# Routing attention and a squared-ReLU feed-forward: moving the rounding of `w_out` between the additions of the first feed-forward

## The chip, the cores and the metric

The kernel runs on one core of a Trainium2 chip. The metric is device time in microseconds (us). The core has a matmul engine (PE, with its weight loads shown as PEld), a vector engine (DVE), an activation engine (ACT), a general engine (POOL) and SP, a sequencer that here only issues DMAs. Each engine works through its own queue in order, and waits on semaphores for the others.

## The reference, cut to what matters

Two blocks follow each other. The first is attention in which a query sees only the keys of its own cluster; the second is a feed-forward whose activation is a squared ReLU:

```python
attn_out = _attn_ref(q, k, v, centroids)            # 4 batches, 8 heads, 768 rows, 64 wide
x = attn_out.transpose(0, 2, 1, 3).reshape(3072, 512)
h = x @ w_in                                        # w_in  512 x 2048
g = np.maximum(h, 0.0) ** 2
out = g @ w_out                                     # w_out 2048 x 512
```

The change concerns only the second block, and there only the first of its four batches.

## The kernel before

**Stages.** The attention runs over 16 pairs of heads (the loop over `p`). Then each of four batches, in the order 1, 2, 3, 0 (`FEED`), goes through `up` (x times `w_in`, squared ReLU, result in the tile `g`) and `down` (`g` times `w_out`, result in `osb` and out).

**Seven products instead of eight.** Both `up` and `down` split their operands into 2 x 2 parts and use a scheme with seven products of sums. `combine` (line 680) runs it: product 1 goes to a PSUM bank and ACT copies it out (line 698); then for products 6, 2, 7, 5, 4, 3 in this order PE fills one bank each, and DVE adds the bank into the result with seven operations (line 694 for the additions, line 520 for the one subtraction, product 4). There are eight banks, used in turn, so PE may be at most eight banks ahead of the engine that empties them. `up` has eight groups `i` of seven products; each product is four matmuls, issued as f32 (line 735). `down` has three groups `i` for each batch; each product is eight matmuls (line 787).

**Sums that the products need.** `w_sums(i)` (line 535) makes four sums `s1` to `s4` of parts of `w_in` on POOL, two groups ahead in the first `up`. Products 5, 6, 7 and 3 of group `i` read `s1`, `s2`, `s3`, `s4`. `w_out_sum(1..4)` (line 761) makes four sums of `w_out` on DVE, once, in the first group of the first `down`. `down` makes two sums of `g`, `s1` and `s2`, and overwrites two quarters of `g` by differences, on DVE.

**Rounding the weights.** Both weight matrices come as 64-bit words that are rounded to a 32-bit form in blocks of 128 x 512. Block `n` takes a DMA into a staging buffer `w_raw` (line 120, on SP's queue), two operations on ACT (`round_1`, lines 128 and 129), three on DVE (`round_2`, lines 135, 138 and 142), and one addition on POOL (`round_3`, line 150). Blocks 0 to 15 are `w_in`, 16 to 31 `w_out`. The attention loop rounds blocks 0 to 14. Block 15 and all of `w_out` are rounded inside the first `up`. There are three staging buffers, and `load_ahead(r)` issues the loads of all blocks below r + 3; a load waits until POOL is done with the block that had its buffer.

**Order.** From the start to the end of the first group of the first `down`, the order on PE, DVE, ACT, POOL and SP is the order of the program (`manual_schedule`). In the first `up`, `rounding(i, 1)` comes behind ACT's copy of product 1 and the squares of the group before: it queues `round_1` for three blocks in groups 0 and 1, for two in the others. `rounding(i, 2)` comes behind all additions of a group (and behind `w_sums(i + 2)` on POOL): it queues `round_2` and `round_3` of the same blocks one after the other, and the next loads. In group 0 it first adds up the last pair's softmax sums (`add_up` on PE, `invert` on DVE, a DMA out and back by `invert` and `spread`, and `finish` on DVE, line 508, which waits for that DMA). `check_sums` (lines 815 to 821) reads all those sums once; its DVE part is placed by the scheduler, and stands right behind `invert` in this trace.

In the other `up`s there is no rounding; DVE does most squares, and `w_sums(i)` is made with its group.

Of the kernel before, what the change touches and what calls it, by code (L numbers as in the profile page):

```python
# [12 lines left out]
U32 = mybir.dt.uint32  # L13
# [5 lines left out]
P = 128  # L19
# [6 lines left out]
def kernel(  # L26
# [18 lines left out]
    FT = DFF // P  # L45
    HP = H // 2
    NB = NCH // 2
    TB = NB * P
# [63 lines left out]
            weights.append((w_in[:, a, cols], w_in64[:, a, cols]))  # L112
    N_IN = len(weights)
    raw_w = {}

    def load_weights(i):
        if i < N_IN + FT:
            src = weights[i][1] if i < N_IN else w_out64[:, i - N_IN]
            raw_w[i] = wstage.tile([P, NW, 2], U32, name="w_raw")
            nc.sync.dma_start(raw_w[i], src)  # L120

    def of_block(i):
# [349 lines left out]
    def add_up(pair, bank):  # L472
        rows = P // 4
        for e in range(2):
            for g in range(2):
                nc.tensor.matmul(  # L476
                    bank[rows * (2 * e + g) : rows * (2 * e + g + 1), 0:TB], lhsT=ups[:, 0:rows],
                    rhs=total[pair][:, e, TB * g : TB * (g + 1)], start=True, stop=True,
                )
        total.pop(pair)  # L480
        sums[pair] = bank
# [37 lines left out]
    def sub(out, a, b, eng=nc.vector):  # L519
        return eng.tensor_tensor(out=out, in0=a, in1=b, op=ALU.subtract)  # L520
# [33 lines left out]

    def load_ahead(rounded):
        nonlocal loaded
        while loaded < min(rounded + 3, N_IN + FT):
            load_weights(loaded)
            loaded += 1

# [96 lines left out]
                    first_sums.append(found)  # L657
            w_early.append(w_sums(len(w_early)))
    att.close()
    load_ahead(NG - 1)  # L660

    w_out_pool = ctx.enter_context(tc.tile_pool(name="w_out_pool", bufs=1, reuse_waits="tile"))

# [2 lines left out]
    banks = fast.enter_context(tc.tile_pool(name="banks", bufs=8, space=PSUM, reuse_waits="tile"))  # L666
    outp = fast.enter_context(tc.tile_pool(name="outp", bufs=2, reuse_waits="tile"))
    gp = fast.enter_context(tc.tile_pool(name="gp", bufs=1, reuse_waits="tile"))

    def bank_tile(width):  # L670
        return banks.tile([P, width], F32, name="bank", tag="bank")
# [5 lines left out]
    ]  # L677
    w_t = {}

    def combine(c, product, width, early=(), behind_copy=None):  # L680
        (c11, c12), (c21, c22) = c
        waiting = {}

        def bank_of(j):
            if j in waiting:
                return waiting[j]
            bank = bank_tile(width)
            product(j, bank)
            return bank

        def add(j, *results):
            bank = bank_of(j)
            for out, to in results:
                nc.vector.tensor_tensor(out=out, in0=bank, in1=to, op=ALU.add)  # L694

        bank = bank_tile(width)
        product(1, bank)
        nc.scalar.copy(out=c11, in_=bank)  # L698
        if behind_copy:
            behind_copy()  # L700
        for j in early:
            waiting[j] = bank_of(j)
        add(6, (c12, c11))
        add(2, (c11, c11))
        add(7, (c21, c12))
        add(5, (c22, c21), (c12, c12))
        sub(c21, c21, bank_of(4))
        add(3, (c12, c12))
# [11 lines left out]
    def up(b, g, rounding=None):  # L720
        with tc.issue_after(last_w_sum[0]) if b == FEED[1] else ExitStack():
            x, t1, t2, t3, t4 = first_sums.pop() if first_sums else list(x_sums(b))[-1]
        waiting = []
        for i in range(F2):
            if rounding is None:
                w_early.append(w_sums(i))
            a, s1, s2, s3, s4 = w_early.pop(0)
            operands = {
                1: (a[0][0], x[0][0]), 2: (a[0][1], x[1][0]), 3: (s4, x[1][1]), 4: (a[1][1], t4),
                5: (s1, t1), 6: (s2, t2), 7: (s3, t3),  # L730
            }

            def product(j, bank):
                for kk in range(H2):
                    nc.tensor.matmul(  # L735
                        bank, lhsT=operands[j][0][:, kk], rhs=operands[j][1][:, kk],
                        start=(kk == 0), stop=(kk == H2 - 1),
                    )

            def behind_copy():  # L740
                if waiting:
                    squares(waiting.pop(), True)
                rounding(i, 1)

            c = [[g[:, f, h] for h in range(2)] for f in (i, F2 + i)]
            combine(c, product, TB, behind_copy=rounding and behind_copy)
            if rounding is None:
                squares(c, False)
                continue
            if i + 1 < F2:  # L750
                waiting.append(c)
            else:
                squares(c, False)
            if i + 2 < F2:
                w_early.append(w_sums(i + 2))
            rounding(i, 2)
        xT.pop(b)

    last_w_sum = [None]

    def w_out_sum(i):
        one, two = {1: (w_q[0][1], w_q[0][0]), 2: (w_q[1][1], w_t.get(1)),
                    3: (w_q[1][1], w_q[0][1]), 4: (w_t.get(2), w_q[1][0])}[i]
        w_t[i] = wtp.tile([P, F2, M2], F32, name=f"w_t{i}")
        last_w_sum[0] = sub(w_t[i], one, two).ins

    def down(b, g):
        for i in range(NB):
            begins = b == FEED[0] and i == 0
            cols = slice(i * P, (i + 1) * P)  # L770
            a = [[g[:, F2 * g2 : F2 * (g2 + 1), h, cols] for g2 in range(2)] for h in range(2)]
            s1, s2 = (sp.tile([P, F2, P], F32, name=f"g_s{j}", tag=f"s{j}") for j in (1, 2))
            nc.vector.tensor_tensor(out=s1, in0=a[1][0], in1=a[1][1], op=ALU.add)
            sub(s2, s1, a[0][0])
            if begins:
                w_out_sum(1)
            else:
                sub(a[1][0], a[0][0], a[1][0])

            def product(j, bank):  # L780
                left, right = {
                    1: (a[0][0], w_q[0][0]), 2: (a[0][1], w_q[1][0]), 3: (a[0][1], w_q[1][1]),
                    4: (a[1][1], w_t.get(4)), 5: (s1, w_t.get(1)), 6: (s2, w_t.get(2)),
                    7: (a[1][0], w_t.get(3)),
                }[j]
                for f in range(F2):
                    nc.tensor.matmul(  # L787
                        bank, lhsT=left[:, f], rhs=right[:, f], start=(f == 0), stop=(f == F2 - 1)
                    )
                if j == 2:  # L790
                    sub(a[0][1], a[0][1], s2)
                    if begins:
                        w_out_sum(2)
                        sub(a[1][0], a[0][0], a[1][0])
                if j == 3 and begins:
                    w_out_sum(3)
                    w_out_sum(4)

            osb = [outp.tile([P, DM], F32, name="osb") for _ in range(2)]
            c = [[osb[h][:, M2 * m : M2 * (m + 1)] for m in range(2)] for h in range(2)]  # L800
            combine(c, product, M2, early=(2, 3) if begins else (2, 4))
            if begins:
                manual.close()
                check_sums()
            last = b == FEED[-1] and i == NB - 1
            for h in (1, 0):
                for cols in (slice(0, M2), slice(M2, DM)) if last and h == 0 else (slice(0, DM),):
                    nc.sync.dma_start(out_view[b, h * NB + i][:, cols], osb[h][:, cols])
# [13 lines left out]
            out=flag[0:1], in0=every, scalar1=UP * float(rows * NG * NBL), scalar2=None, op0=ALU.is_lt  # L822
        )

    to_round = list(range(N_IN - 1, N_IN + FT))

    def rounding(i, stage):
        if stage == 2 and i == 0:
            add_up(NG - 1, bank_tile(TB))
            invert(NG - 1)  # L830
            spread(NG - 1)
            finish(NG - 1)
        if stage == 2 and i == 1:
            ending.close()
        blocks = to_round[: 3 if i < 2 else 2]
        if stage == 1:
            for n in blocks:
                if n >= N_IN:
                    round_1(n)
            return  # L840
        for n in blocks:
            round_2(n)
            round_3(n)
            load_ahead(n + 1)
        del to_round[: len(blocks)]

    for n, b in enumerate(FEED):
        g = gp.tile([P, FT, 2, TB], F32, name="g")
        up(b, g, None if n else rounding)
        if n == 0:  # L850
            staging.close()
            wtp = fast.enter_context(
                tc.tile_pool(name="wtp", bufs=1, side="right", reuse_waits="tile")
            )
            xT[0] = xp.tile([P, KT, S], F32, name="xT")
            nc.sync.dma_start(xT[0], x_far)
        down(b, g)
        if n == 0:
            again = nc.values_load(flag[0:1, 0:1], min_val=0, max_val=1)
# [191 lines left out]
```

## Time and profile before

| what | before |
|---|---|
| median of 3 runs | 919.5 us (919.38 to 921.3) |
| the profiled execution, its own time | 917.96 us |
| its span in the trace | 916.2 us, so 1.8 us lie outside it |
| PE / PEld / DVE / ACT / POOL busy | 98% / 63% / 63% / 34% / 16% |
| attention | start to 320.8 us |
| first `up` | 320.80 to 399.15 us: 56 products of PE and one small sum |
| first group of the first `down` | 399.15 to 427.41 us |
| second `up` | from 475.98 us |

Busy shares are means over the span. A view by stages shows more: of the first feed-forward, ten slices of 10 us each have

```profile
core 0: us, PE busy (x) PEld busy (x) DVE busy (x) ACT busy (x) POOL busy (x), PEclk, DMA share, GB/s
320.00:330.00 10.00, 10.00 (x37) 5.52 (x32) 5.82 (x8) 3.22 (x6) 5.26 (x5) 1.00 0.16 52
330.00:340.00 10.00, 10.00 (x38) 5.64 (x38) 4.53 (x10) 4.23 (x9) 2.82 (x4) 1.00 0.13 40
340.00:350.00 10.00, 6.93 (x17) 3.65 (x16) 9.65 (x15) 2.49 (x4) 7.35 (x7) 0.83 0.46 159
350.00:360.00 10.00, 10.00 (x32) 5.81 (x31) 9.58 (x17) 7.87 (x16) 7.23 (x7) 1.00 0.46 143
...
390.00:400.00 10.00, 10.00 (x33) 6.08 (x32) 9.55 (x19) 7.65 (x16) 3.28 (x3) 1.00 0.26 90
400.00:410.00 10.00, 6.28 (x30) 5.10 (x28) 9.83 (x12) 0.37 (x1) 2.20 (x1) 1.00 0.45 158
```

Each row is a stretch of the span; the columns are its length, then busy time and instructions of each engine, the clock that PE was granted (1.00 is full), and the DMA engines' share and rate. DVE is half idle up to 340 us and then busy without a break; PE is short of work in two of the slices, and its clock is below 1.00 in one.

### The profile page before, as it was taken

To read this page: it belongs to the slowest core of one execution; us is meant where nothing else is said; L and a number is where in the kernel's file an instruction comes from. 1 tells how busy PE (TensorE), PEld (TensorE's weight loads), DVE (VectorE), ACT (ScalarE), POOL (GpSimd) and SP (SyncE) were. 2 spreads that over 40 slices of the span, in tenths; PEclk is the share of its full clock that TensorE was granted. 3 is DMA by queue.
4 is the path that set the end of the run, shared out by engine and by line. 5 is a ranking of instruction groups with operands and counts; after the bars stand their busy time and mean duration, and the time that the engine had idled before them with its cause. 6 is when DMAs were issued, how large, how long until landed. Compare 5 with 4: busy or idle time off the path is not lost.

```text
span 916.2 us, 11745 instructions
## 1 busy us (share of the span) xinstructions
PE 900.2 (98%) x4543; PEld 578.9 (63%) x4543; DVE 580.9 (63%) x930; ACT 315.3 (34%) x457; POOL 146.1 (16%) x168
## 2 busy tenths in 40 slices
PE   8999999999999999989999999999999999999997
PEld 5444444444444455558885568886558887557886
DVE  5798888888888959996326565224565333656321
ACT  5876677766775536830001110001110000111000
POOL 0000100001000347620022310013320003240000
PEclk9999999999999999999999999999999999999999
DMA  7677787777663114330000000000000000000000
GB/s 260 164 192 217 223 202 205 193 222 186 176 169 102 41 46 156 118 113 24 24 24 0 1 0 12 16 19 23 1 1 0 24 24 24 0 1 0 24 24 27
DMA packets 98482, 75.03 MB, mean 82 GB/s; under 512 B 54666, under 2 KB 89074, under 8 KB 98162
## 3 DMA queue, kind: packets, MB, share of 16 engines
q1 hardware_dynamic: 91474, 64.33, 24.7%
q10 hardware_dynamic: 6944, 9.86, 3.4%
q8 instruction: 38, 0.62, 0.3%
q14 instruction: 26, 0.21, 0.1%
HBM read 43.83 MB, written 19.34 MB: 69 GB/s over the span
## 4 chain that ended last, share of the span: by engine, by line
PE 92%; DVE 6%; issue 1%; DMA 1%; ACT 0%; POOL 0%; SPq 0%; DVEq 0%; POOLq 0%
PE bank L787 31%; PE bank L735 29%; PE sc L424 12%; PE av_a L457 9%; PE av_b L457 4%; PE sc L433 3%; PE sc L320 1%; PE sc L476 1%; DVE g L694 1%; DVE w_raw L138 1%; DVE w_raw L135 1%; DVE total L443 1%; PE sc L169 0%; DMA rb<-far_r 0%; DVE xT L508 0%
## 5 line engine op out<-in xcount | busy, mean ns | idle before, releaser
L694 DVE TENSOR_TENSOR g<-bank,g 128x384 f32<-128x384 f32 x192 | 103.2, 555 | 94.7 <-PE bank L735 91.3
L440 ACT ACTIVATE ex<-sc 128x1024 f32<-128x1024 f32 x144 | 144.4, 1026 | 39.0 <-PE sc L424 34.1
L424 PE MATMUL sc<-qkT 64*128 64x512 f32 (+1 forms) x768 | 150.6, 484 | 0.0
L787 PE MATMUL bank<-w_out,g 128*128 128x256 f32 x576 | 127.3, 379 | 3.7 <-DVE g L520 3.7
L787 PEld LDWEIGHTS bank<-w_out,g 128*128 128x128 f32 x576 | 109.2, 190 | 19.9 <-DVE g L520 4.1
L694 DVE TENSOR_TENSOR osb<-bank,osb 128x256 f32<-128x256 f32 x72 | 29.4, 422 | 134.6 <-PE bank L787 124.1
L735 PE MATMUL bank<-xT,w_in 128*128 128x384 f32 x256 | 93.9, 490 | 3.1 <-DVE g L694 3.1
L735 PE MATMUL bank<-xT,w_s 128*128 128x384 f32 x256 | 94.2, 491 | 0.0
L735 PE MATMUL bank<-x_t,w_s 128*128 128x384 f32 x256 | 93.0, 486 | 0.0
L424 PEld LDWEIGHTS sc<-qkT 64*128 64x128 f32 x768 | 65.9, 188 | 41.9 <-issue 30.1
L787 PE MATMUL bank<-w_t,g 128*128 128x256 f32 x384 | 86.8, 379 | 0.0
L787 PE MATMUL bank<-w_t,g_s 128*128 128x256 f32 x384 | 86.8, 379 | 0.0
L457 PE MATMUL av_a<-ex,v_raw 128*64 128x512 f32 x384 | 85.9, 596 | 0.0
L443 DVE TENSOR_TENSOR total<-total,ex 128x1024 f32<-128x1024 f32 x64 | 78.7, 1229 | 6.5
L540 POOL TENSOR_TENSOR w_s<-w_in 128x256 f32<-128x256 f32 x32 | 24.7, 772 | 347.2 <-PE bank L787 226.4
L698 ACT COPY osb<-bank 128x256 f32<-128x256 f32 x12 | 4.5, 373 | 219.1 <-PE bank L787 219.1
L787 PEld LDWEIGHTS bank<-w_t,g_s 128*128 128x128 f32 x384 | 73.0, 190 | 9.9
L787 PEld LDWEIGHTS bank<-w_t,g 128*128 128x128 f32 x384 | 73.0, 190 | 9.9
L698 ACT COPY g<-bank 128x384 f32<-128x384 f32 x32 | 15.3, 477 | 172.5 <-PE bank L735 172.5
L735 PEld LDWEIGHTS bank<-xT,w_in 128*128 128x128 f32 x256 | 48.3, 190 | 37.3 <-DVE g L694 4.0
L735 PEld LDWEIGHTS bank<-xT,w_s 128*128 128x128 f32 x256 | 49.2, 192 | 34.6 <-issue 1.2
L150 POOL TENSOR_TENSOR w_in<-w_in,w_raw 128x512 int32<-128x512 int32 x16 | 22.4, 1400 | 302.2 <-DVE w_in L142 285.8
(128 smaller groups left out, 1015.6 us busy)
## 6 DMA issues: line engine op xcount, KB each, us to landing
words<-flat SPq DMA_DIRECT2D x28, 384.0 KB
w_raw<-in_moe_w_in_dram SPq DMA_DIRECT2D x16, 512.0 KB
w_raw<-in_moe_w_out_dram SPq DMA_DIRECT2D x16, 512.0 KB
v_raw<-in_v_dram SPq DMA_DIRECT2D x16, 384.0 KB
rb<-far_r SPq DMA_DIRECT2D x32, 192.0 KB
out_dram<-osb SPq DMA_DIRECT2D x23, 256.0 KB
k_raw<-in_k_dram ACTq DMA_DIRECT2D x13, 384.0 KB
q_raw<-in_q_dram ACTq DMA_DIRECT2D x12, 384.0 KB
```

The costliest lines, as they stand in the source:

```text
L135: nc.vector.scalar_tensor_tensor(out=lo, in0=hi, scalar=0x80000000, in1=lo, op0=ALU.bitwise_and, op1=ALU.bitwise_or)
L150: nc.gpsimd.tensor_tensor(out=dst, in0=dst, in1=lo, op=ALU.add)
L424: nc.tensor.matmul(sc[i][:, e, cols], lhsT=qkT[pair][rows, NCH + c], rhs=qkT[pair][rows, n.start // P : n.stop // P], start=first, stop=no ...
L433: nc.tensor.matmul(sc[i][:, e, cols], lhsT=ohT[pair][rows, 1, c * P : (c + 1) * P], rhs=ohT[pair][rows, 0, columns(i)], start=first, stop= ...
L440: nc.scalar.activation(out=ex[i], in_=sc.pop(i), func=ACT.Exp, scale=SCALE)
L443: eng.tensor_tensor(out=out, in0=a, in1=b, op=ALU.add)
L457: nc.tensor.matmul(bank[D * e : D * (e + 1), 0 : n.stop - n.start], lhsT=raw_v[pair][:, e, c], rhs=ex[i][:, e, cols], start=c == 0, stop=c ...
L540: nc.gpsimd.tensor_tensor(out=s1, in0=a[1][0], in1=a[1][1], op=ALU.add)
L694: nc.vector.tensor_tensor(out=out, in0=bank, in1=to, op=ALU.add)
L698: nc.scalar.copy(out=c11, in_=bank)
L735: nc.tensor.matmul(bank, lhsT=operands[j][0][:, kk], rhs=operands[j][1][:, kk], start=(kk == 0), stop=(kk == H2 - 1),)
L787: nc.tensor.matmul(bank, lhsT=left[:, f], rhs=right[:, f], start=(f == 0), stop=(f == F2 - 1))
```

## The change

- **Blocks by group.** The 17 blocks are now three a group in groups 0 to 4 and two in group 5; groups 6 and 7 round none. `Rounding.between(i, j)` is called behind the addition of product `j`: the group's first block goes behind the addition of product 6, its second behind that of 7, its third behind that of 3. Each is `round_2`, `round_3` and the load for the block six further on.
- **`round_1` a group earlier.** `Rounding.prepare(i)`, at the place of the old first stage, queues ACT's part for the blocks of group i + 1 (in group 0 for those of groups 0 and 1).
- **Six staging buffers.** A second pool of three, `stage_2`, opens after the attention's pools are closed; blocks alternate between the pools in threes. `load_ahead` runs six blocks ahead from there on.
- **Moved tail of the attention.** `add_up`, `invert` and `spread` of the last pair stay behind group 0, now behind its three blocks; `finish` moves behind group 2.
- **`w_out`'s sums.** Sums 1, 2 and 3 are made in the first `up`, behind the additions (6, 7), (6, 3) and (7, 7) of (group, product); only sum 4 stays in the first `down`, behind product 2. The subtraction on `a[1][0]` comes there at once, as in the other groups.
- **The first `down`'s order on PE** is 1, 2, 5, 7, 3, 6, 4 instead of 1, 2, 3, 6, 7, 5, 4.

```diff
@@ -112,11 +112,13 @@
             weights.append((w_in[:, a, cols], w_in64[:, a, cols]))
     raw_w = {}
+    stage_2 = None
 
     def load_weights(i):
         if i < N_IN + FT:
             src = weights[i][1] if i < N_IN else w_out64[:, i - N_IN]
-            raw_w[i] = wstage.tile([P, NW, 2], U32, name="w_raw")
+            pool = stage_2 if i > N_IN and (i - N_IN + 1) // 3 % 2 else wstage
+            raw_w[i] = pool.tile([P, NW, 2], U32, name="w_raw")
             nc.sync.dma_start(raw_w[i], src)
 
     def of_block(i):
@@ -554,7 +556,7 @@
 
     def load_ahead(rounded):
         nonlocal loaded
-        while loaded < min(rounded + 3, N_IN + FT):
+        while loaded < min(rounded + (6 if stage_2 else 3), N_IN + FT):
             load_weights(loaded)
             loaded += 1
 
@@ -657,7 +659,6 @@
                     first_sums.append(found)
             w_early.append(w_sums(len(w_early)))
     att.close()
-    load_ahead(NG - 1)
 
     w_out_pool = ctx.enter_context(tc.tile_pool(name="w_out_pool", bufs=1, reuse_waits="tile"))
 
@@ -666,6 +667,10 @@
     banks = fast.enter_context(tc.tile_pool(name="banks", bufs=8, space=PSUM, reuse_waits="tile"))
     outp = fast.enter_context(tc.tile_pool(name="outp", bufs=2, reuse_waits="tile"))
     gp = fast.enter_context(tc.tile_pool(name="gp", bufs=1, reuse_waits="tile"))
+
+    staging_2 = ExitStack()
+    stage_2 = staging_2.enter_context(tc.tile_pool(name="stage_2", bufs=3, reuse_waits="tile"))
+    load_ahead(NG - 1)
 
     def bank_tile(width):
         return banks.tile([P, width], F32, name="bank", tag="bank")
@@ -677,7 +682,7 @@
     ]
     w_t = {}
 
-    def combine(c, product, width, early=(), behind_copy=None):
+    def combine(c, product, width, early=(), behind_copy=None, behind_add=None):
         (c11, c12), (c21, c22) = c
         waiting = {}
 
@@ -692,6 +697,8 @@
             bank = bank_of(j)
             for out, to in results:
                 nc.vector.tensor_tensor(out=out, in0=bank, in1=to, op=ALU.add)
+            if behind_add:
+                behind_add(j)
 
         bank = bank_tile(width)
         product(1, bank)
@@ -740,10 +747,13 @@
             def behind_copy():
                 if waiting:
                     squares(waiting.pop(), True)
-                rounding(i, 1)
+                rounding.prepare(i)
 
             c = [[g[:, f, h] for h in range(2)] for f in (i, F2 + i)]
-            combine(c, product, TB, behind_copy=rounding and behind_copy)
+            combine(
+                c, product, TB, behind_copy=rounding and behind_copy,
+                behind_add=rounding and (lambda j: rounding.between(i, j)),
+            )
             if rounding is None:
                 squares(c, False)
                 continue
@@ -753,7 +763,7 @@
                 squares(c, False)
             if i + 2 < F2:
                 w_early.append(w_sums(i + 2))
-            rounding(i, 2)
+            rounding.behind(i)
         xT.pop(b)
 
     last_w_sum = [None]
@@ -772,10 +782,7 @@
             s1, s2 = (sp.tile([P, F2, P], F32, name=f"g_s{j}", tag=f"s{j}") for j in (1, 2))
             nc.vector.tensor_tensor(out=s1, in0=a[1][0], in1=a[1][1], op=ALU.add)
             sub(s2, s1, a[0][0])
-            if begins:
-                w_out_sum(1)
-            else:
-                sub(a[1][0], a[0][0], a[1][0])
+            sub(a[1][0], a[0][0], a[1][0])
 
             def product(j, bank):
                 left, right = {
@@ -790,15 +797,11 @@
                 if j == 2:
                     sub(a[0][1], a[0][1], s2)
                     if begins:
-                        w_out_sum(2)
-                        sub(a[1][0], a[0][0], a[1][0])
-                if j == 3 and begins:
-                    w_out_sum(3)
-                    w_out_sum(4)
+                        w_out_sum(4)
 
             osb = [outp.tile([P, DM], F32, name="osb") for _ in range(2)]
             c = [[osb[h][:, M2 * m : M2 * (m + 1)] for m in range(2)] for h in range(2)]
-            combine(c, product, M2, early=(2, 3) if begins else (2, 4))
+            combine(c, product, M2, early=(2, 5, 7, 3) if begins else (2, 4))
             if begins:
                 manual.close()
                 check_sums()
@@ -822,36 +825,50 @@
             out=flag[0:1], in0=every, scalar1=UP * float(rows * NG * NBL), scalar2=None, op0=ALU.is_lt
         )
 
-    to_round = list(range(N_IN - 1, N_IN + FT))
-
-    def rounding(i, stage):
-        if stage == 2 and i == 0:
-            add_up(NG - 1, bank_tile(TB))
-            invert(NG - 1)
-            spread(NG - 1)
-            finish(NG - 1)
-        if stage == 2 and i == 1:
-            ending.close()
-        blocks = to_round[: 3 if i < 2 else 2]
-        if stage == 1:
-            for n in blocks:
+
+    class Rounding:
+        blocks = [[N_IN - 1 + 3 * i + j for j in range(3)] for i in range(F2)]
+
+        def of(self, i):
+            return [n for n in self.blocks[i] if n < N_IN + FT] if i < F2 else []
+
+        def prepare(self, i):
+            for n in self.of(i) + self.of(1) if i == 0 else self.of(i + 1):
                 if n >= N_IN:
                     round_1(n)
-            return
-        for n in blocks:
-            round_2(n)
-            round_3(n)
-            load_ahead(n + 1)
-        del to_round[: len(blocks)]
+
+        def between(self, i, j):
+            n = dict(zip((6, 7, 3), self.of(i))).get(j)
+            if n is not None:
+                round_2(n)
+                round_3(n)
+                load_ahead(n + 1)
+            elif (i, j) in SUMS:
+                w_out_sum(SUMS[i, j])
+
+        def behind(self, i):
+            nonlocal wtp
+            if i == 0:
+                add_up(NG - 1, bank_tile(TB))
+                invert(NG - 1)
+                spread(NG - 1)
+            if i == 2:
+                finish(NG - 1)
+            if i == 5:
+                staging_2.close()
+                ending.close()
+                staging.close()
+                wtp = fast.enter_context(
+                    tc.tile_pool(name="wtp", bufs=1, side="right", reuse_waits="tile")
+                )
+
+    SUMS = {(6, 7): 1, (6, 3): 2, (7, 7): 3}
+    wtp = None
 
     for n, b in enumerate(FEED):
         g = gp.tile([P, FT, 2, TB], F32, name="g")
-        up(b, g, None if n else rounding)
+        up(b, g, None if n else Rounding())
         if n == 0:
-            staging.close()
-            wtp = fast.enter_context(
-                tc.tile_pool(name="wtp", bufs=1, side="right", reuse_waits="tile")
-            )
             xT[0] = xp.tile([P, KT, S], F32, name="xT")
             nc.sync.dma_start(xT[0], x_far)
         down(b, g)
```

## The prediction

> **What bounds the kernel now.** I read the page's chain of waits first: it runs through PE for nine tenths of the span.
>
> ```profile
> PE 92%; DVE 6%; issue 1%; DMA 1%; ACT 0%; POOL 0%; SPq 0%; DVEq 0%; POOLq 0%
> ```
>
> So only time in which PE stands still or runs slowly can be won. The timeline of PE (start, us, operation, count, and in brackets the idle time before it and its releaser) says where that is, inside the stage that the change touches:
>
> ```profile
> 341.23 1.45 PE L735 MATMUL bank<-x_t,w_s 128*128 128x384 f32 x4
> 345.75 2.12 PE L735 MATMUL bank<-xT,w_in 128*128 128x384 f32 x4 [3.07 <-DVE g L694]
> 347.67 2.63 PE L735 MATMUL bank<-xT,w_s 128*128 128x384 f32 x4
> 350.13 1.46 PE L735 MATMUL bank<-x_t,w_s 128*128 128x384 f32 x4
> ...
> 399.15 7.07 PE L787 MATMUL bank<-w_out,g 128*128 128x256 f32 x32
> 409.95 3.72 PE L787 MATMUL bank<-w_out,g 128*128 128x256 f32 x16 [3.72 <-DVE g L520]
> ```
>
> A product of `up` begins every 1.29 us, one of `down` every 3.45. From 320.80 to 427.41 (106.6 us) PE has 56 products of the one (72.2), `add_up` (0.8) and 7 of the other (24.2): 97.2. It **loses 9.4 us**: 3.2 waiting for a bank at 342.5, 1.8 in the two products behind, which take 1.92 and 2.46 instead of 1.29 at a lower clock, 3.9 waiting for DVE's subtraction at 406, some 0.5 in handovers. After 427.41 nothing is left to win here.
>
> Both waits are DVE's. Its timeline has the first cause, and then a group of two blocks:
>
> ```profile
> 337.13 1.60 DVE L508 SCALAR_TENSOR_TENSOR xT<-xT,rb 128x384 f32<-128x384 f32 x2 [3.47 <-DMA rb<-far_r]
> ...
> 359.05 0.55 DVE L694 TENSOR_TENSOR g<-bank,g 128x384 f32<-128x384 f32 x1
> 359.52 1.24 DVE L135 SCALAR_TENSOR_TENSOR w_raw<-w_raw 128x512 uint32<-128x512 uint32 x1
> 360.80 0.43 DVE L138 TENSOR_SCALAR w_raw<-w_out 128x512 f32<-128x512 f32 x1
> 361.26 0.43 DVE L142 TENSOR_SCALAR w_out<-w_raw 128x512 uint32<-128x512 uint32 x1
> 361.61 0.69 DVE L135 SCALAR_TENSOR_TENSOR w_raw<-w_raw 128x512 uint32<-128x512 uint32 x1
> 362.33 1.40 DVE L138 TENSOR_SCALAR w_raw<-w_out 128x512 f32<-128x512 f32 x1
> 363.76 0.43 DVE L142 TENSOR_SCALAR w_out<-w_raw 128x512 uint32<-128x512 uint32 x1
> ```
>
> From 331.8 DVE waits 5.3 us for the reciprocals' DMAs (0.4 of it is L815), then rounds three blocks, and empties no bank until 345.15. From there it never idles. The same line takes 0.69 or 1.24, 0.43 or 1.40; POOL's timeline shows why.
>
> ```profile
> 357.29 0.73 POOL L540 TENSOR_TENSOR w_s<-w_in 128x256 f32<-128x256 f32 x1
> 358.10 0.73 POOL L520 TENSOR_TENSOR w_s<-w_s,w_in 128x256 f32<-128x256 f32 x1
> 358.79 0.73 POOL L520 TENSOR_TENSOR w_s<-w_in 128x256 f32<-128x256 f32 x1
> 359.48 0.73 POOL L520 TENSOR_TENSOR w_s<-w_in,w_s 128x256 f32<-128x256 f32 x1
> 361.77 1.67 POOL L150 TENSOR_TENSOR w_out<-w_out,w_raw 128x512 int32<-128x512 int32 x1 [1.56 <-DVE w_out L142]
> 364.27 1.30 POOL L150 TENSOR_TENSOR w_out<-w_out,w_raw 128x512 int32<-128x512 int32 x1 [0.82 <-DVE w_out L142]
> ```
>
> The L135 at 359.52 ends 0.55 late, as the last `w_s` sum runs; the L138 at 362.33 0.97 late, behind the L150 that slipped in between L135 and L138. They take turns, one instruction each. The adds out of PSUM (L694) don't suffer.
>
> **Prices on DVE.** Seven bank operations: 3.65 (355.87 to 359.52). A block alone: 0.72 + 0.46 + 0.35 = 1.53. Waits: 1.5 for two blocks, now.
>
> **The change, part by part.**
>
> *`finish` two groups later.* The 5.3 us of DVE idling go. SP's order matters: the loads of blocks 21, 22, 23 now stand ahead of the reciprocals' DMAs, and the last waits for block 17's L150 (about 334.2). By the 1.40, 0.45 and 3.31 us that the chain shows for these DMAs they land near 340; `finish` comes near 355, so that costs nothing. L815 needs the first of them, at about 336: between 0, if the scheduler puts it in a gap, and 2.4 us, if right behind `invert` as now. I take its 0.44, since what follows is no longer a wait for a DMA.
>
> *Rounding between the adds, three a group.* The first block now starts one add (0.54) behind the previous group's third, while POOL still has that block's L150 (1.30) and, behind it, four `w_s` sums. With turns taken, from the rows above: first block's L135 waits 0.83 for the L150, its L138 0.41 and its L142 0.44 for a `w_s` sum each; second block, two adds later, 0.15 and 0.97; third, four adds later, nothing. Sum 2.8. A group then costs DVE 3.65 + 3 x 1.53 + 2.8 = **11.0 us against PE's 9.03**. Group by group, from the add at 323.7: group 0 has 3.65 + 4.6 + 1.0 of waits + 0.85 for `invert` + 0.44 = 10.5; group 1, where POOL is less behind, 10.0; group 2, with `finish` (1.6 and a wait of about 1.1), 13.6; group 3, 9.8; group 4, 11.0. Group 5 starts at 378.6.
>
> *What stops PE then.* Before its bank does, the `w_s` sum: product 6 is second in a group and needs `s2`, the second of the four. POOL gets to it in the group before, behind that group's first L135 and in turn with its L138: about 3.5 us into the group (add 0.54, wait 0.83, L135 0.53, first sum 0.6 and its turn 0.4, second sum 0.7). So product 6 of group 6 starts at 382.1. Unhindered it would at 320.80 + 6 x 9.03 + 0.8 + 1.29 + 0.3 = 377.4. **New loss 4.7 us**, taken as three stops of some 2 us, plus 0.4 of handovers. Here lies the trade: loss moves from two big stops into a lag of DVE.
>
> *Groups 5 to 7 and the first `down`.* From there PE needs 13 x 1.29 = 16.8 and is at `down` at 398.9. Two blocks in group 5 (8.2 + waits), then 3.65 + 2 x 2.21 = 8.1 in group 6 and 3.65 + 2.21 + 1.4 of squares in group 7, all under or near 9.03, bring DVE to `down`'s first sum at 403.5. The sums cost 2.28 as now (L520). `s1` is ready at 404.7; product 5 wants it at 398.9 + 6.9 = 405.8, so that the order 1, 2, 5 covers it with 1.1 to spare. `a[1][0]` (407.1) and `a[0][1]` (408.3) are wanted at 409.3 and 412.7. The wait of 3.9 is gone; what is late next is `s1`.
>
> *`round_1` early, six buffers, loads.* ACT has per group 0.4 of copy, 4 of squares, 3 x 1.16 of `round_1`: 7.9, under DVE's 11. Blocks 17 to 20 are loaded at once at 321.8, 2.1 MB. Nearest rows: 240 GB/s with two in flight (346 to 350 us), so 331 to 332; alone each takes 3.47 from issue to use, so 335.7. Block 20's `round_1` stands ahead of ACT's copy for group 1: cost 0 to 3 us; I take 0, by the row with several in flight. Later loads have a whole group.
>
> *Sum.* 9.4 lost before, 5.1 after: 4.3. The same addition, applied to the kernel before, gives 8.1 us for a group of two that takes 8.24; over the five slow groups I give back 0.6. **Gain 3.7 us**: the profiled execution of 917.96 (span 916.2, 1.8 around it) would take 914.3, the median 919.5 about 915.8.
>
> [...] The change sets twelve sums and L150s right beside rounding, where before only the last sum met it. By the rows, with the part of a POOL instruction that is already over taken off, waits are 2.8 a group; if each met a whole one (0.73, 0.73, 1.30, and 0.83 as before) it is 3.6 or more, and 0.8 more in four groups leaves 0.5 of gain. I take the rows, as they show the turns.
>
> [...] The row has one of 3.07 that cost 1.8 and one of 3.72 that cost nothing. [...] I take 0.
>
> **Rivals.**
>
> *DVE keeps up.* If L150 and sums fall beside adds rather than rounding, a group costs 8.2 to 9: no stop is left, gain 9.4 less handovers, **910.5**. For it: L694 never waits. Against: L150 follows its own block by 0.13, and only one add separates it from the next. Chance 0.2.
>
> *POOL's sums become the bound (slower).* PE's product 6 waits for the whole `w_s` tile, two sums more, each behind a DVE turn (+1.6), and each wait is a whole instruction (12.1 a group). It decides from 12 us a group on, where the loss reaches the 9.4 of before; with both it is near 11, **921**. For it: four sums of 0.7 behind each third block. Against: the partial waits measured. Chance 0.18.
>
> *The first stop stays.* Block 20 comes late (3 us), ACT's copy for group 1 with it, and the gain shrinks to 0.6: **918.9**. Nothing in the trace shows four loads at once at this place. Chance 0.14; the forecast has 0.48.
>
> **How the numbers follow.** Forecast's own range is 913 to 918. Reaching into the rivals until two in ten are left: 910.8 to 920.2. A change under 0.2% (1.84 us) can't be told from none. Faster by more: 0.46 of the forecast, 0.2, and a fifth of the late block: 0.69. Slower by more: most of the POOL rival, 0.17. Same: 0.14.
>
> **What would show it.** After: no DVE idle before `finish`, no 3 us stop near 342, none at L787 near 406. Stops of 1 to 2.5 us at product 6 of groups 4, 5, 6, released by POOL; L135 at 1.3 or more in first blocks, L138 near 1.4 in second ones; add of product 6 of group 5 near 378.6. It is wrong if groups of three take DVE under 9.5 or over 12 us, or if PE waits for DVE's `s1` in `down`.

## The result, and the profile after

| | before | after |
|---|---|---|
| median of six runs | 919.48 us (919.31 to 921.3) | **913.09 us** (912.51 to 913.43) |
| ratio after / before | | 0.9924, 95% interval 0.9912 to 0.9937 |
| profiled execution, its own time | 917.96 us | 913.43 us |
| span | 916.2 us | 911.6 us |
| the stage: start of the first `up` to the end of the first group of the first `down` | 320.80 to 427.41: 106.6 us | 321.38 to 422.93: 101.55 us |
| of it over PE's 97.2 us of work | 9.4 us | 4.4 us |

The change gains 6.4 us; 3.7 were forecast. What follows the stage takes as long as it did: 916.2 - 427.41 = 488.8 us before, 911.6 - 422.93 = 488.7 after. So in the two profiled executions (4.5 us apart) nothing is gained outside the stage: it is 5.1 us shorter, and begins 0.6 later. The page's chain of waits for the kernel after has a point less of DVE, a point more of ACT, and no DMA:

```profile
PE 92%; DVE 5%; issue 1%; ACT 1%; POOL 0%; DVEq 0%; POOLq 0%
```

The table of slices of 10 us, for after (length, then busy time and instructions of PE, PEld, DVE, ACT, POOL, then PE's granted clock, the DMA share and GB/s):

```profile
340.00:350.00 10.00, 10.00 (x33) 5.89 (x32) 9.83 (x19) 7.89 (x16) 6.55 (x7) 1.00 0.65 190
...
370.00:380.00 10.00, 8.95 (x28) 5.24 (x28) 9.83 (x16) 4.66 (x10) 7.01 (x8) 1.00 0.00 0
380.00:390.00 10.00, 8.55 (x28) 4.90 (x27) 9.76 (x16) 4.44 (x9) 9.02 (x10) 1.00 0.01 2
...
400.00:410.00 10.00, 10.00 (x48) 8.81 (x47) 9.39 (x11) 0.37 (x1) 0.00 (x0) 1.00 0.36 146
```

The two slices in which PE was short of work, 340 to 350 and 400 to 410, are full now, at full clock. What PE lacks it lacks between 360 and 390. PE's timeline names both places (start, us, operation, and in brackets the idle time before it and its releaser); the third line is `down`'s product 5, the first reader of `s1`:

```profile
371.05 1.56 PE L742 MATMUL bank<-x_t,w_s 128*128 128x384 f32 x4 [1.70 <-POOL w_s L522]
...
381.79 1.56 PE L742 MATMUL bank<-x_t,w_s 128*128 128x384 f32 x4 [1.45 <-POOL w_s L522]
...
405.57 3.62 PE L794 MATMUL bank<-w_t,g_s 128*128 128x256 f32 x16
```

Both stops are product 6, of groups 5 and 6, waiting for its `w_s` sum; neither waits for a bank. Product 5 of `down` has no bracket: it waits for nothing. The queue behind the first stop is seen on DVE, in the group that starts at 367.53:

```profile
367.53 0.55 DVE L699 TENSOR_TENSOR g<-bank,g 128x384 f32<-128x384 f32 x1
367.99 1.54 DVE L137 SCALAR_TENSOR_TENSOR w_raw<-w_raw 128x512 uint32<-128x512 uint32 x1
369.57 0.84 DVE L140 TENSOR_SCALAR w_raw<-w_out 128x512 f32<-128x512 f32 x1
370.45 0.83 DVE L144 TENSOR_SCALAR w_out<-w_raw 128x512 uint32<-128x512 uint32 x1
...
372.13 0.97 DVE L137 SCALAR_TENSOR_TENSOR w_raw<-w_raw 128x512 uint32<-128x512 uint32 x1
373.14 1.40 DVE L140 TENSOR_SCALAR w_raw<-w_out 128x512 f32<-128x512 f32 x1
```

and beside it on POOL's timeline:

```profile
367.69 1.30 POOL L152 TENSOR_TENSOR w_out<-w_out,w_raw 128x512 int32<-128x512 int32 x1 [2.10 <-DVE w_out L144]
368.94 1.18 POOL L542 TENSOR_TENSOR w_s<-w_in 128x256 f32<-128x256 f32 x1
370.20 0.79 POOL L522 TENSOR_TENSOR w_s<-w_s,w_in 128x256 f32<-128x256 f32 x1
```

POOL's L152 for the third block of the group before starts 0.16 behind the start of the add, so that DVE's first L137 stands behind it (1.54 instead of 0.69), and POOL's first `w_s` sum behind that L137 (1.18 instead of 0.73). The second sum ends at 371.0, 3.5 us into the group, and at 371.05 product 6 starts.

### The profile page after: what moved, and what is told of

Read it like the earlier page. It is cut to its first block, busy times and chain, and to the rows that moved or that the text cites. A ratio compares the mean times of both kernels' runs of the same rounds, so it can differ in the third digit from the quotient of the medians.

```text
span 911.6 us, 11728 instructions
## 1 busy us (share of the span) xinstructions
PE 899.4 (99%) x4543; PEld 578.8 (63%) x4543; DVE 581.7 (64%) x930; ACT 316.2 (35%) x457; POOL 150.1 (16%) x168
## 4 chain that ended last, share of the span: by engine, by line
PE 92%; DVE 5%; issue 1%; ACT 1%; POOL 0%; DVEq 0%; POOLq 0%
PE bank L794 32%; PE bank L742 28%; PE sc L426 12%; PE av_a L459 9%; PE av_b L459 4%; PE sc L435 3%; PE sc L322 1%; DVE w_raw L137 1%; PE sc L478 1%; DVE g L699 1%; DVE w_raw L140 1%; DVE total L445 1%; DVE xT L510 0%; PE sc L171 0%; PE sc L265 0%
## 5 line engine op out<-in xcount | busy, mean ns | idle before, releaser
L542 POOL TENSOR_TENSOR w_s<-w_in 128x256 f32<-128x256 f32 x32 | 26.7, 835 | 351.3 <-PE bank L794 235.4
L742 PEld LDWEIGHTS bank<-x_t,w_s 128*128 128x128 f32 x256 | 48.4, 190 | 37.9 <-POOL w_s L522 4.8
L152 POOL TENSOR_TENSOR w_in<-w_in,w_raw 128x512 int32<-128x512 int32 x16 | 22.1, 1378 | 296.4 <-DVE w_in L144 296.4
```

The source lines that it names most:

```text
L152: nc.gpsimd.tensor_tensor(out=dst, in0=dst, in1=lo, op=ALU.add)
L542: nc.gpsimd.tensor_tensor(out=s1, in0=a[1][0], in1=a[1][1], op=ALU.add)
L742: nc.tensor.matmul(bank, lhsT=operands[j][0][:, kk], rhs=operands[j][1][:, kk], start=(kk == 0), stop=(kk == H2 - 1),)
```

## The experiments

Their medians, with the ratio to before on the same chip:

| run | edit | us | ratio, 95% interval |
|---|---|---|---|
| e1 | before, with `finish` two groups later | 915.55 | 0.9951 (0.9934 to 0.9968) |
| e2 | after, with all of `w_out`'s sums in `down`, and before's order of products there | 914.91 | 0.9946 (0.9929 to 0.9962) |
| e3 | after, with `w_sums` ahead of the third block | 911.57 | 0.9911 (0.9894 to 0.9927) |
| e4 | after, with the three blocks in a row | 918.59 | 0.9987 (0.9976 to 0.9998) |
| e5 | after, with three buffers, `round_1` in its own group | 915.46 | 0.9953 (0.9937 to 0.9969) |
| e6, e6b | before, unchanged, profiled twice more | 919.67, 919.38 | |
| e7 | e3, with `finish` behind group 5 | 910.77 | 0.9898 (0.9884 to 0.9913) |
| e8 | e4, with group 0 interleaved | 915.59 | 0.9949 (0.9936 to 0.9963) |
| e9 | e8, with `finish` behind group 5 | 916.56 | 0.9959 (0.9946 to 0.9973) |

Before's own median beside these runs was 919.5 to 919.9, against 919.48 beside after, so a difference of 0.4 us between a run and after (913.09) means nothing.

### e1: `finish` alone

```diff
@@ before: rounding(i, 2)
             spread(NG - 1)
+        if stage == 2 and i == 2:
             finish(NG - 1)
-        if stage == 2 and i == 1:
             ending.close()
```

> The kernel before, with nothing moved but finish of the last pair (behind group 2 instead of group 0). Theory A (the first stop of PE is DVE's idle wait for the reciprocals' DMA, and most of the gain is that this wait goes): the stop near 342 and the slow clock behind it go (5.0 us), the stop of 3.7 at the first down's third product stays; about 914.5. Rival B (the interleaving and the six buffers bring the gain, the moved finish is incidental, since DVE still has two groups of three blocks one after the other): under 1.5 us of gain, 918 or more, with a stop of PE for a bank in group 2 or 3.

The bank stop near 342 and the slow clock behind it are gone: PE is busy without a break from 338 to 350, and its clock is 1.00 from 340 to 350. The stop for DVE's subtraction in `down` stays (PE's timeline of e1):

```profile
406.32 5.38 PE L787 MATMUL bank<-w_out,g 128*128 128x256 f32 x16 [3.72 <-DVE g L520]
411.54 3.62 PE L787 MATMUL bank<-w_t,g_s 128*128 128x256 f32 x16
```

This time the clock falls behind it (0.58 and 0.57 in the two stretches of 2 us from 406 to 410), so that the product takes 5.22 to the next start instead of 3.45. Moving this one step out of the way of the banks is worth 3.95 us (919.5 to 915.55) by itself.

### e2: the sums of `w_out` back in `down`

```diff
@@ after: down, in the first group
-            sub(a[1][0], a[0][0], a[1][0])
+            if begins:
+                w_out_sum(1)
+            else:
+                sub(a[1][0], a[0][0], a[1][0])
...
-                        w_out_sum(4)
+                        w_out_sum(2)
+                        sub(a[1][0], a[0][0], a[1][0])
+                if j == 3 and begins:
+                    w_out_sum(3)
+                    w_out_sum(4)
...
-            combine(c, product, M2, early=(2, 5, 7, 3) if begins else (2, 4))
+            combine(c, product, M2, early=(2, 3) if begins else (2, 4))
...
-    SUMS = {(6, 7): 1, (6, 3): 2, (7, 7): 3}
+    SUMS = {}
```

> The changed kernel, with all four sums of w_out and the order of products put back into the first down as before. Theory A (the second stop came from DVE arriving late at down, with a block of group 7 still to round; the sums' place alone matters little): DVE reaches down's first sum about 3 us earlier than with the sums in groups 6 and 7, the third product waits under 1 us; 913 to 914. Rival B (the sums in down are what cost the 3.9 us): the wait of 3.5 to 4 us comes back, about 917.

PE's two stops for POOL are the same (1.70, 1.45). The third product of `down` waits 1.32, not 3.7 (PE's timeline of e2):

```profile
407.68 3.72 PE L797 MATMUL bank<-w_out,g 128*128 128x256 f32 x16 [1.32 <-DVE g L522]
```

So most of before's stop came from DVE's being late into `down` with its last blocks, and less than half from what was queued there: DVE begins the first sum of `g` 2.3 us behind PE's start of `down`, not 4.0, and the second takes it 1.23 us, not 2.12. The place of `w_out`'s sums, together with the order of products that goes with it, is worth 1.8 us (914.91 to 913.09).

### e3: POOL's `w_s` sums ahead of the third block

```diff
@@ after: up
+            def behind_add(j):
+                if j == 3 and i + 2 < F2:
+                    w_early.append(w_sums(i + 2))
+                rounding.between(i, j)
...
-            if i + 2 < F2:
-                w_early.append(w_sums(i + 2))
             rounding.behind(i)
```

> The changed kernel, with w_sums(i + 2) queued on POOL ahead of the group's third block instead of behind it. Theory A (the two stops of PE left, 3.5 us, are the second w_s sum standing behind the third block's addition on POOL): both stops go, the DVE lag stays at 10.5 to 11 us a group, and PE then waits 1 to 2 us for s1 in down instead; about 911.5. Rival B (DVE's lag is the bound whatever POOL's order, and the banks stop PE in the same place): PE waits for DVE out of a bank in groups 4 to 6, 913, no change.

Both stops for `w_s` go. In their place PE waits four times for a bank, 0.28 to 0.40 each (1.4 together); two of the four, from PE's timeline of e3:

```profile
371.56 1.53 PE L742 MATMUL bank<-xT,w_s 128*128 128x384 f32 x4 [0.33 <-DVE g L699]
...
374.77 1.56 PE L742 MATMUL bank<-x_t,w_in 128*128 128x384 f32 x4 [0.40 <-DVE g L699]
```

The stage takes 100.07 us instead of 101.55. The stop at `s1` that was expected in exchange did not come. So the two stops of after were the order on POOL: the sums sat behind the third block's addition. They were worth 1.5 us, for behind them DVE's own lag is next.

### e4: the three blocks in a row

```diff
@@ after: class Rounding
         def between(self, i, j):
-            n = dict(zip((6, 7, 3), self.of(i))).get(j)
-            if n is not None:
-                round_2(n)
-                round_3(n)
-                load_ahead(n + 1)
-            elif (i, j) in SUMS:
+            if (i, j) in SUMS:
                 w_out_sum(SUMS[i, j])
@@ behind(self, i)
+            for n in self.of(i):
+                round_2(n)
+                round_3(n)
+                load_ahead(n + 1)
             if i == 0:
```

> The changed kernel, with the three blocks of a group rounded one behind the other after the addition of product 3 and after w_sums, as in the kernel before, all else kept. Theory A (the interleaving itself saves DVE nothing: 10.7 us for three blocks back to back against 10.85 interleaved): a group costs 10.6 to 10.9 us of DVE, product 6 waits for no sum; 911 to 914. Rival B (the interleaving frees banks sooner and is the source of the gain): stops for a bank of 2 us or more return in groups 2 to 5, 916 or more.

I expected little of this and was wrong: without the interleaving, nearly the whole gain is lost (918.59). It isn't that a group costs DVE more: its first L137 of groups 1 and 2 start at 345.76 and 355.94, 10.2 apart; in after the same two are 10.1 apart (334.81, 344.95). Two things are lost. DVE's timeline of e4 has the first at the start of `up`, the second in group 2:

```profile
326.98 0.56 DVE L699 TENSOR_TENSOR g<-bank,g 128x384 f32<-128x384 f32 x1 [0.73 <-PE bank L742]
...
331.32 0.85 DVE L137 SCALAR_TENSOR_TENSOR w_raw<-w_raw 128x512 uint32<-128x512 uint32 x1
...
363.02 2.66 DVE L510 SCALAR_TENSOR_TENSOR xT<-xT,rb 128x384 f32<-128x384 f32 x2
365.61 2.79 DVE L699 TENSOR_TENSOR g<-bank,g 128x384 f32<-128x384 f32 x5
```

In group 0 DVE is as fast as PE delivers, waits before nearly every add, and begins its first block at 331.32; after puts that block into the gaps, from 324.79. Between 320 and 330 us DVE is busy 6.39 us here and 8.70 in after. The work not done there is done later, when DVE is the late one. A smaller loss adds to it: the reciprocals come 6 us later, and L818 in group 1 waits 1.44 for their DMA, where it waits for none in after. Then from 355.94 to 365.61 DVE rounds three blocks and does `finish` without emptying a bank, and PE runs through its eight banks (PE's timeline of e4):

```profile
366.21 2.93 PE L742 MATMUL bank<-xT,w_in 128*128 128x384 f32 x4 [4.01 <-DVE g L699]
368.93 2.76 PE L742 MATMUL bank<-xT,w_s 128*128 128x384 f32 x4
```

A stop of 4.01 and a slow clock (0.50 from 368 to 372), as at 342 before. By the starts of the products behind the stop (2.72, 2.56 and 1.58 apart for 1.29) the clock costs 3.0 us, over half of what e4 loses.

### e8: interleaved in group 0 only; e9: and `finish` behind group 5

```diff
@@ e4: class Rounding, between(self, i, j)
-            if (i, j) in SUMS:
+            n = dict(zip((6, 7, 3), self.of(i))).get(j) if i == 0 else None
+            if n is not None:
+                round_2(n)
+                round_3(n)
+                load_ahead(n + 1)
+            elif (i, j) in SUMS:
...
-            for n in self.of(i):
+            for n in self.of(i) if i else []:
@@ e9 as well: behind(self, i)
-            if i == 2:
-                finish(NG - 1)
             if i == 5:
+                finish(NG - 1)
```

> The back-to-back kernel, with the three blocks of group 0 alone put between the additions as in the changed kernel; groups 1 to 5 round behind their last addition. Theory A (interleaving pays where DVE would wait for PE between additions, in group 0, 3 us, and nowhere else; later on it costs, since POOL's sums then stand in the way of rounding and of product 6): a group costs DVE 10.2 to 10.7 us from 334 on, PE's lead of eight banks lasts to the end, no stop over 1 us; 909 to 911. Rival B (the early banks of every group are what the interleaving gains): the stop of 4 us for a bank in group 3 and its slow clock stay, 916 or more.

> The same with finish behind group 5 instead of group 2. Theory A: DVE's lag comes later, so no stop for a bank is left; the total of DVE's work is the same, so s1 in down may be late by up to 1 us; 909 to 910.5. Rival B (the stop for a bank comes from the rounding in one piece, 7 us, not from finish): the stop in group 3 to 5 stays, 913 or more.

These split e4's loss. Interleaving in group 0 alone brings 3.0 of its 5.5 us back (918.59 to 915.59). It isn't all of it, against what was expected: in group 1 DVE again waits 0.66 and 0.73 for PE before two adds and 1.12 for a DMA, and three bank stops of 1.84, 0.87 and 1.42 are left, the longest in group 4 (PE's timeline of e8):

```profile
363.10 1.56 PE L742 MATMUL bank<-xT,w_in 128*128 128x384 f32 x4 [1.84 <-DVE g L699]
```

With `finish` out of group 2 these don't go, they come later (0.95, 1.44, 1.51, then 0.58 and 1.03 in `down`), and e9 is no faster than e8. (The profiled execution of e9, 918.21 us, is the slowest of its five; it has a slow clock in `down` besides, 0.50 from 410 to 412.) So the gaps of group 0 account for 3.0 of the 5.5 us. The other 2.5 come from interleaving groups 1 to 5. Whether that is the gaps of group 1 again (2.5 us of waits) or the banks that come free in the middle of a group, these runs don't separate.

### e5: three staging buffers

```diff
@@ after: load_weights
-            pool = stage_2 if i > N_IN and (i - N_IN + 1) // 3 % 2 else wstage
+            pool = wstage
...
-        while loaded < min(rounded + (6 if stage_2 else 3), N_IN + FT):
+        while loaded < min(rounded + 3, N_IN + FT):
@@ prepare
-            for n in self.of(i) + self.of(1) if i == 0 else self.of(i + 1):
+            for n in self.of(i):
```

> The changed kernel with three staging buffers; loads run three blocks ahead and round_1 comes in its own group, since the buffers aren't free earlier. Theory A (the early round_1, which six buffers allow, is what lets a block stand behind the first addition of a group): DVE's first block of each group waits for ACT, which has 4 us of squares and 1.2 of round_1 ahead of it, some 4 us a group in groups 1 to 5; 925 to 935. Rival B (the buffers are incidental, ACT and the loads have time anyway): 913 to 915.

The collapse of the first theory did not come; the loss against after is 2.4 us. DVE's timeline of e5 has the one long wait, in group 1:

```profile
337.74 0.36 DVE L816 SCALAR_TENSOR_TENSOR seen<-seen 128x192 f32<-128x192 f32 x1 [3.64 <-DMA far_r<-seen]
```

ACT's `round_1` for the block behind it ended at 337.6 as well, so both were late. After that DVE waits for ACT's `round_1` three times, 0.83 to 0.84 us each, and no more: it runs behind PE, which gives ACT time. PE's timeline of e5 has what the 3.6 became:

```profile
372.45 1.99 PE L740 MATMUL bank<-x_t,w_s 128*128 128x384 f32 x4 [2.02 <-POOL w_s L522]
374.24 2.75 PE L740 MATMUL bank<-xT,w_in 128*128 128x384 f32 x4
```

A stop only 0.3 longer than in after, but with a slow clock behind it (0.50 from 374 to 376), which costs 1.7 by the starts of this and the next two products.

### e6 and e6b: the kernel before, twice more

Nothing is edited. The timed runs of before lie roughly at three levels, near 918, 919.5 and 921, and the profile of the prediction (917.96) was of the lowest. These two are of the middle one; none of the upper was profiled, so what makes that one stays open.

> The kernel before, unchanged, for another profile. Theory A (its times of about 917.8, 919.5 and 921.3 differ by how much slow clock follows its two stops): this run's time goes with the PE time lost behind the stops: at 919.5 about 1.7 us more of slow products than in the first profile (1.8), at 921.3 about 3.4 more. Rival B (the levels come from elsewhere, such as the attention or the DMAs): the products behind the stops take the same as in the first profile, and the difference lies outside 320 to 428 us.

> As the run before it: the unchanged kernel once more, since one profile may fall on the level that is known already.

PE's timeline of e6 at the stop in `down`:

```profile
410.30 5.41 PE L787 MATMUL bank<-w_out,g 128*128 128x256 f32 x16 [3.70 <-DVE g L520]
415.55 3.62 PE L787 MATMUL bank<-w_t,g_s 128*128 128x256 f32 x16
```

and a slice of it, in the columns of the table above:

```profile
412.00:414.00 2.00, 2.00 (x6) 1.55 (x6) 2.00 (x3) 0.00 (x0) 0.00 (x0) 0.50 0.00 0
```

The stop is that of the first profile (3.70 for 3.72). But the next product starts 5.25 behind this one, not 3.55: the clock was at half, and 1.8 us more than the usual 3.45 went. e6b has the same (3.71, 5.25, 0.50). Their stages take 108.6 and 108.7 us, against the first profile's 106.6: 1.7 of the 2 us is this clock, the rest a first stop of 3.41 and 3.47 instead of 3.07. The clock over the whole run says it too: in the thirteen runs of before that stood beside e1 to e4 it was 0.997 in the two at 917.7 and 918.0 us, and 0.994 to 0.996 in the others; in all six runs of after it was 0.999 or 1.000.

### e7: a faster version

```diff
@@ e3: behind(self, i)
-            if i == 2:
-                finish(NG - 1)
             if i == 5:
+                finish(NG - 1)
```

> The kernel with w_sums ahead of the third block, and finish (3.25 us of DVE there, with its waits) moved from group 2 to group 5. Theory A (the lag of DVE is the bound of what is left, and a lag that comes later stops PE less): the four small waits for a bank in groups 4 and 5 (1.4 us, 1.9 with their handovers) go, s1 in down still comes in time; about 909.7. Rival B (the lag is only moved, PE then waits for a bank in group 6 or for s1 in down): 911.5, no change.

The `w_s` sums first, and `finish` where only two blocks are left to round: one bank stop of 0.24 and one of 0.59 at `s1` remain, the stage takes 98.95 us, 1.8 over PE's work, and the median is 910.77, below both kernels and between the two forecasts. The stop at `s1` on PE's timeline of e7:

```profile
403.31 3.72 PE L797 MATMUL bank<-w_t,g_s 128*128 128x256 f32 x16 [0.59 <-DVE g_s L786]
```

`finish` took DVE 2.7 us in group 2 of after, and 2.29 here, at 384.73, where its lag is nearly over; what is late next is DVE at `down`.

## Why the prediction was right, and where its size was not

- **What bounds it, and the trade.** Right: the two DVE stops went, DVE no longer idles before `finish`, and a lag of DVE over groups 1 to 5 came in their place. e1 shows the first stop's part alone, e2 how the second divides between DVE's late arrival and the sums queued in `down`.
- **DVE's groups.** The starts were forecast at 13.4, 23.4, 37.0, 46.8 and 57.8 us into the stage; they are 12.96, 23.10, 36.56, 46.15 and 56.91. The group shown takes 10.76 for 11.0. Its waits for POOL are 0.85 + 0.41 + 0.40 in the first block, 0.28 + 0.97 in the second: 2.9, where the rows gave 2.8 and whole instructions 3.6. The first of them, 0.85, is behind an L152 of 1.30 that had begun 0.30 ahead of the L137 (367.69 and 367.99): less than the whole instruction was waited for.
- **What stops PE.** Right in kind: product 6 waits for the second `w_s` sum, 3.5 us into DVE's group. Of three stops only two came (1.86 and 1.61 with the handover); in group 4 product 6 came 0.04 late. Product 6 of group 6 starts 60.4 into the stage, forecast 61.3. Here the loss is 4.4 for 5.1.
- **The clock behind the new stops.** Right for after: 1.00 in every slice. That stops of 2 us cost no clock was the author's estimate: no run of before shows it, and the two stops it rested on, 3.07 and 3.72, had cost 1.8 and nothing. In its place the runs showed 1.70 and 1.45 (after) at no cost, 1.91 (e5) at none, and 2.02 (e5) at 1.7. The new stops came out shorter than the 2 us of the forecast; so the term was right in part by luck. The last section has more of such stops.
- **Loads, L815, `down`.** The four loads at once were not late: of ACT's `round_1` for them only the first waits (1.21 us, to 325.80), the others follow without a wait to 330.96, and ACT's copy for group 1 is at 332.98, after a wait of 2.01 for its own product. L815 (now L818) ran at 340.02 between an L137 and its L140, without a wait for its DMA, and put the L140 off by about 0.2 (forecast 0.44). `s1` is ready at 403.9 for 405.57, 1.7 to spare (forecast 1.1).
- **The rivals.** DVE did not keep up (its groups of three take 9.6 to 10.8, and 13.5 with `finish`; PE's 9.03), POOL's sums did not cost more than the old stops, and block 20 was not late.

**The step that failed is a term of the sum**: "9.4 lost before". It was measured right in the one execution there was, and the text took the same 3.7 us off the median. In e6 and e6b the loss is 11.4 and 11.5, since the stop that "cost nothing" costs 1.7 more by the clock there, and the first stop is 0.3 to 0.4 longer. On the profiled execution the forecast was 914.3 and after took 913.43, 0.9 off: 0.75 from stops that were smaller, 0.6 from the give-back that was not due, less 0.6 by which the stage began later (321.38 for 320.80); 0.1 came behind the stage. The rest of the miss is 1.8 of 2.7 us. Of it 1.5 is before's median over its profiled execution (919.48 for 917.96); e6 and e6b put that down to the clock behind a stop that the change took away, and that was not priced. The other 0.3 is after's median under its own profiled execution, and stays open. The median of 913.09 lies at the very edge of the forecast's own range, 913 to 918.

## What to carry to other kernels

Work that is off the critical path belongs into the gaps of an engine while that engine still waits for others: without the interleaving 5.5 of the 6.4 us were gone (e4), though it saved DVE nothing within a group, and the first group alone brought 3.0 back (e8). Before an engine's total is taken as the bound, look at the order on a second engine that holds it up (here POOL, by 2.9 us in a group of DVE's): two stops of after, 1.70 and 1.45 us, hung on what stood ahead of four sums on POOL. And profile the kernel before more than once, since the same stop cost its own length in one profile (3.72 us) and half as much again in two (3.70 in e6 and 3.71 in e6b, each with 1.8 of slow clock behind it).

## What the hardware showed that was not expected

- **The length of a stop did not settle what the clock did.** 3.7 us cost nothing more in the first profile of before, and 1.7 to 1.8 in e1, e6 and e6b. Stops of 1.84 (e8) and 1.91 (e5) cost nothing, one of 2.02 (e5) cost 1.7, one of 4.01 (e4) 3.0. In e9 a stop of 1.03, with one of 0.58 just ahead of it, cost 1.8 (the clock was at 0.50 from 410 to 412 us), while 1.04 at the same product cost nothing in e4 and e8. The traces' record of the granted clock shows when it changes. In the first profile of before it falls to 0.50 at 346.61, rises at 350.03, and falls again at 913.23, when PE's work is over; in e6 it falls at 346.79 and 411.64 and rises at 350.20 and 415.05. So the slow stretches inside these two runs last 3.41 us each, and from a rise to the next fall it is 563.20 = 165 x 3.413 in before and 61.44 = 18 x 3.413 in e6. By the slices, the slow stretches of e1, e5, e6b and e9 last 3.4 us as well, that of e4 6.8. 3.41 us at a clock of 0.50 is 1.7 us less work (an estimate from these two figures), near the 1.7 to 1.8 measured. Here is the stop in `down` in stretches of 3.41 us counted from those changes, in the columns of the table above, first of before and then of e6:

```profile
404.64:408.05 3.41, 1.58 (x8) 0.97 (x6) 3.41 (x2) 0.00 (x0) 0.83 (x1) 1.00 0.06 25
408.05:411.47 3.42, 1.52 (x7) 1.37 (x8) 3.42 (x3) 0.00 (x0) 0.00 (x0) 1.00 0.00 0
411.47:414.88 3.41, 3.41 (x18) 3.00 (x17) 3.41 (x3) 0.00 (x0) 0.00 (x0) 1.00 0.00 0
...
404.81:408.22 3.41, 1.79 (x9) 1.17 (x7) 3.41 (x2) 0.00 (x0) 1.02 (x1) 1.00 0.10 40
408.22:411.64 3.42, 1.34 (x6) 1.21 (x7) 3.42 (x3) 0.00 (x0) 0.00 (x0) 1.00 0.00 0
411.64:415.05 3.41, 3.41 (x10) 2.70 (x9) 3.41 (x3) 0.00 (x0) 0.00 (x0) 0.50 0.00 0
```

Before's stop falls almost evenly on two stretches, with PE busy 1.58 and 1.52 us in them, and the clock stays at 1.00. The same stop in e6 lies 0.2 us later in them, PE is busy only 1.34 in the second, and the clock falls to 0.50 at its end. Counted in the same way on PE's timelines from 320 to 425 us, each run from its own changes of the clock, the 3.41 us ahead of each fall have PE busy 0.86 (before), 0 (e1), 0.32 (e4), 1.39 (e5), 0.66 and 1.34 (e6), 0.07 and 0.75 (e6b), and 1.79 in e9, where they hold the two short stops. The least that no fall followed is the 1.52 of before; e6 has one of 1.79 as well, its first above, as much as e9's. So the busy time of such a stretch does not settle it alone. No run moved a stop on purpose, and why e9's clock fell is open.
- **Loads issued together ran much faster than the nearest row had it.** The four blocks of 512 KB at the start of after moved at 381 and 406 GB/s in the stretches of 2 us from 324 to 328, against the 240 that the forecast took from two in flight:

```profile
324.00:326.00 2.00, 2.00 (x8) 1.14 (x7) 1.65 (x3) 0.79 (x3) 2.00 (x3) 1.00 0.98 381
326.00:328.00 2.00, 2.00 (x8) 1.21 (x7) 1.97 (x5) 1.95 (x4) 1.17 (x2) 1.00 1.04 406
```
